# Two-part stores of the expert outputs, and weight conversion dealt out around each g in the FFN

## The chip, the cores and the metric

The kernel runs on 1 core of one Trainium2 chip. The metric is the device time of one execution in microseconds (us). The engines are named as in the profile: PE (TensorE matmul), PEld (TensorE weight load), DVE (VectorE), ACT (ScalarE), POOL (GpSimd), SP (SyncE, which only issues transfers here).

## The reference

Three layers follow each other on 2304 tokens of width 512.

```python
def phi(x):                                   # attention, 4 x 8 heads, 576 positions, head width 64
    proj = x @ w_phi                          # to 128 features
    proj = proj - max(abs(proj))
    return concat([exp(proj), exp(-proj)])
num = phi(q) @ (phi(k).T @ v); den = phi(q) @ sum(phi(k)) + 1e-6
x = num / den                                 # 2304 x 512

e_idx = argmax(x @ w_gate)                    # one of 8 experts for each token
for e in range(8):                            # expert stage, hidden width 1024
    h = maximum(x[mask] @ w1[e], 0)
    out[mask] = gate_w * sigmoid(x @ w_output_gate)[e] * (h @ w2[e])

h = x @ w_in                                  # FFN: 512 -> 2048 -> 512
out = (h * sigmoid(h)) @ w_out                # w_in and w_out come as float64
```

## The kernel before, in words

**Split operands.** Matrix products of the expert stage and the FFN are made from operands in two parts, a rounded high part (`h`) and a low part (`l`, the value minus its high part): high x high, high x low and low x high, three matmuls for one. The high part is an ACT copy into the rounded type (`F32R`), the low part a DVE subtraction.

**Expert stage** (class `Moe`). Tokens are sorted by expert into tiles of 256 slots, at most 16; a tile that is at most half full runs in a small form of 128. In this input 13 tiles run, numbers 0 to 12. For a tile t, `first` makes the hidden layer (96 matmuls, L754), `turn(t+1)` transposes the next tile's tokens, and `second` makes the output (96 matmuls, L781). `second_out` (small: the end of `second_small`) copies the result from PSUM into `y[t % 2]` by ACT, and `store` writes it by one DMA from SP's queue into the DRAM tensor `yT`, whose columns are tokens in expert order. Around that, `new_first` and `new_second` split the next expert's weights (ACT and DVE, L653 and L654), `scale` multiplies the gathered tokens (L683), `gather(t+2)` fetches tokens by an indirect DMA from POOL's queue (L670), and `side_work` converts one piece of the FFN's weights per tile. `after(t)` is called behind each tile: behind tile 8 (`SURE - 1`) it starts loading the first chunk of `yT`, behind tile 9 it splits that chunk and loads the next.

**FFN** (function `ffn`). `yT` is read in 6 chunks of 384 tokens, each twice, so there are 12 visits, v = 0 to 11. The hidden width of 2048 is cut into 4 quarters q. A step is a pair (v, q), 24 in all: steps 0 to 5 do quarter 0 for all chunks, steps 6 to 11 do quarters 1, 2 and 3 for visits 6 and 7 in turn, and then each of visits 8 to 11 does its three quarters. A step has 4 groups f, so there are 96 groups; they are called ups here, numbers 0 to 95. For each up, `up` runs 12 matmuls into a PSUM tile `fph` (L1000, two such tiles), ACT makes the sigmoid (L1002), DVE multiplies to g (L1003), ACT rounds g to `gh` (L1004), DVE makes `gl` (L1005). Behind each up, `down` runs the 9 matmuls (L1017) that belong to the up four places before. So PE alternates 12 and 9 matmuls.

The FFN's weights are float64 in DRAM, loaded as `raw` pieces of 128 x 512, and 24 pieces are converted inside the FFN: quarter 1 `i` (4 pieces), quarter 1 `o` (4), and so on to quarter 3, whose parts are written over the tiles of quarter 0 and bear their names, `i0` and `o0`. A piece takes an ACT magnitude (L888), five DVE instructions (`bits`, L894 to L898), a DVE addition (`add`, L903), an ACT copy (`high`, L906) and a DVE subtraction (`low`, L910). `fetch` issues the seven DVE instructions for one piece in one go, behind ups f = 0 and f = 2 of a step (in steps 7 to 10 behind f = 0, 2 and 3). Quarter q = 1 `i` is needed by up 24, `o` by the downs behind up 28, quarter 2 by ups 32 and 36, quarter 3 by ups 40 and 44. The program is in written order on each engine (`manual_schedule`), so an instruction that waits holds all that stands behind it on its engine. Visits are loaded into one staging tile `yst` by SP and split by `ready.next` (ACT L940, DVE L941, twice each per visit), behind f = 1 of the last step before a new visit.

Of the kernel before, what the change touches and what calls it, by code (L numbers as in the profile page):

```python
# [7 lines left out]
F32 = mybir.dt.float32  # L8
F32R = mybir.dt.float32r
# [5 lines left out]
ALU = mybir.AluOpType  # L15
# [586 lines left out]
class Moe:  # L602
# [14 lines left out]
    def open(self, c):  # L617
        tc = self.tc
        sp = c.enter_context(tc.tile_pool(name="m_s", bufs=1, reuse_waits="tile"))
        pt, ph, py = (c.enter_context(tc.tile_pool(name=n, bufs=1, space=PSUM, reuse_waits="tile")) for n in ("m_pt", "m_ph", "m_py"))  # L620
        self.hh, self.hl = (sp.tile([128, FC, TW], F32R, name=n) for n in ("hh", "hl"))
        self.y = self.ring(sp, "y", [128, KC, TW], 2)
# [107 lines left out]
    def second_small(self, t):  # L730
        nc, w, y = self.nc, self.w, self.y[t % 2]
# [10 lines left out]
        nc.scalar.copy(y[:, :, 0:128], q)  # L742
        self.store(t, 128)
# [24 lines left out]
    def store(self, t, n):  # L768
        co = self.nc.values_load(self.r["coff"][0:1, t:t + 1], engines=[ENG.SP], min_val=0, max_val=NTOK) if t else 0
        self.nc.sync.dma_start(out=self.yT[:, :, bass.ds(co, n)] if t else self.yT[:, :, 0:n], in_=self.y[t % 2][:, :, 0:n])  # L770

# [14 lines left out]
    def second_out(self, t):  # L786
        for g in range(2):
            self.nc.scalar.copy(self.y[t % 2][:, 2 * g:2 * g + 2], self.result[g])
        self.store(t, TW)

    def run(self, route, side_load, side_work, after):
        tc, nc = self.tc, self.nc
        side_load(0)
        side_load(1)
        self.first(0, self.y[1], (0,))
        route.slots(self.turned[0])
        self.first(0, self.y[1], (2, 4, 6))
        route.tokens(self.turned[1])
# [67 lines left out]
class Weights:  # L866
# [22 lines left out]

    def bits(self, pool, i, bufs):  # L890
        V, mag, (low, high) = self.nc.vector, self.mag[i], self.words(i)
        val = self.val[i] = pool.tile([128, 512], F32, name="val", bufs=bufs)
        bits = val.bitcast(I32)
        V.tensor_scalar(mag, mag, MAG_LO, MAG_HI, op0=ALU.max, op1=ALU.min)  # L894
        V.tensor_scalar(bits, mag.bitcast(I32), 3, 0x3FFFFFF8, op0=ALU.logical_shift_left, op1=ALU.bitwise_and)  # L895
        V.scalar_tensor_tensor(out=bits, in0=high, scalar=-0x40000000, in1=bits, op0=ALU.bitwise_and, op1=ALU.bitwise_or)  # L896
        V.tensor_scalar(mag.bitcast(I32), bits, -0x800000, None, op0=ALU.bitwise_and)  # L897
        V.scalar_tensor_tensor(out=mag, in0=low.bitcast(U32), scalar=2.0**-52, in1=mag, op0=ALU.mult, op1=ALU.mult)  # L898
        self.raw.pop(i)

    def add(self, i, eng):
# [11 lines left out]
class Ready:  # L913


    def __init__(self, nc, sp, yT):
        self.nc, self.sp, self.yT, self.parts = nc, sp, yT, {}
        self.pools = [sp, sp]
        self.st = sp.tile([128, KC, CN], F32, name="yst", bufs=1)

    def load(self, v):
        ch = v % NCH
        self.nc.sync.dma_start(out=self.st, in_=self.yT[:, :, ch * CN:(ch + 1) * CN])

    def room(self, v):
        self.parts[v] = [self.pools[v % 2].tile([128, KC, CN], F32R, name=n, bufs=1) for n in ("yh", "yl")]

    def next(self, v):

        self.room(v)  # L930
        self.split(v)
        if v + 1 < 2 * NCH:
            self.load(v + 1)

    def split(self, v):
        st = self.st
        yh, yl = self.parts[v]
        for kc in range(0, KC, 2):
            s = slice(kc, kc + 2)
            self.nc.scalar.copy(yh[:, s], st[:, s])  # L940
            self.nc.vector.tensor_sub(yl[:, s], st[:, s], yh[:, s].bitcast(F32))  # L941


def ffn(tc, r, weights, first_pool, fetch_pool, ready, out):

    nc = tc.nc
    V = nc.vector
    QC = GC // 4
    with ExitStack() as c, tc.manual_schedule():
        fp = c.enter_context(tc.tile_pool(name="f_f", bufs=1, reuse_waits="tile"))  # L950
# [6 lines left out]

        ready.pools[1] = sp
        rooms = [("i", 1, fp, "i1"), ("o", 1, wp, "o1"), ("i", 2, wp, "i2"), ("o", 2, wp, "o2")]
# [7 lines left out]
        todo = [(n, q, p) for q in range(1, 4) for n in "io" for p in range(KC)]  # L967
        at = [0]

        def load(n):  # L970
            weights.load(*((sp, todo[n], 1) if n % 3 == 2 else (fetch_pool, todo[n], 2)))

        def fetch():

            n = at[0]
            at[0] += 1
            if n + 1 < len(todo):
                weights.magnitude(sp, todo[n + 1], 3)
            if 2 <= n < len(todo) + 2:
                weights.high(todo[n - 2])  # L980
            if n < len(todo):
                weights.bits(sp, todo[n], 3)
                if n + 3 < len(todo):
                    load(n + 3)
            if 1 <= n < len(todo) + 1:
                weights.add(todo[n - 1], V)
            if 2 <= n < len(todo) + 2:
                weights.low(todo[n - 2], V)

        gts, accs = {}, {}  # L990

        def up(v, q, f):
# [10 lines left out]
            V.tensor_mul(g, p, g)  # L1003
            nc.scalar.copy(gh, g)  # L1004
            V.tensor_sub(gl, g, gh.bitcast(F32))  # L1005

        def down(v, q, f, i):
# [21 lines left out]
        steps += [(NCH + v, q) for v in range(2, NCH) for q in range(1, 4)]  # L1029
        first = {}  # L1030
        for n, (v, q) in enumerate(steps):
            first.setdefault(v, n)
        ready.next(1)
        load(2)
        for n, (v, q) in enumerate(steps):
            if n == NCH + 1:
                room("i", 3, first_pool, "i0")
                room("o", 3, first_pool, "o0")
            for f in range(QC):
                up(v, q, f)  # L1040
                if n == 0 and f == QC - 1:
                    weights.magnitude(sp, todo[0], 3)
                    fetch()
                if n and f in ((0, 2, 3) if NCH < n < NCH + 5 else (0, 2)):
                    fetch()
# [9 lines left out]
def build(tc, qT, kT, v, w_phi, w_gate, w_ogate, w1, w2, w_in, w_out, out, dbg=None):  # L1055
    nc = tc.nc
    with ExitStack() as c:
        cp = c.enter_context(tc.tile_pool(name="consts", bufs=1))
        dr = c.enter_context(tc.tile_pool(name="dram", bufs=1, space=bass.MemoryType.DRAM))
        xs = dr.tile([NTOK, XW], F32, name="xs")  # L1060
        yT = dr.tile([128, KC, NTOK + TW], F32, name="yT")
        k = make_consts(tc, cp)
# [8 lines left out]
        with ExitStack() as e:  # L1071
            with ExitStack() as m:
# [49 lines left out]
                def after(t):  # L1122
                    if t == SURE - 1:
                        cs.close()
                        yp = e.enter_context(tc.tile_pool(name="f_y", bufs=1, side="right", reuse_waits="tile"))
                        ready.append(Ready(nc, yp, yT))
                        ready[0].load(0)
                        ready[0].room(0)
                        ready.append(yp)
                        for p in range(2):  # L1130
                            weights.load(yp, ("i", 1, p), 2)
# [9 lines left out]
            with tc.using_default_side("left"):  # L1141
                ffn(tc, r, weights, ep, ready[1], ready[0], out)
        if dbg is not None:
            for n, a in dbg.items():
                nc.sync.dma_start(out=a, in_={**r, "xs": xs, "yT": yT}[n])

# [56 lines left out]
```

## Time and profile before

| what | value |
|---|---|
| median of 3 runs | 908.86 us (905.67 to 909.38) |
| the profiled execution, its own time | 907.69 us |
| its span, first to last instruction | 905.7 us |
| expert stage, from its first second-layer matmul to the last store's issue | about 200 to 477 us |
| FFN, first matmul to the end | 480.27 to 905.7 us |
| mean granted TensorE clock | 0.979 |

The time of an execution is longer than its span by what lies outside the first and the last instruction (2.0 us here). Times in the rows further down count from the start of the span.

### The profile page before, as it was taken

The numbers are of one execution on the slowest core, as the hardware profiler recorded it, in microseconds if no ns is written. First come the engines' busy times: TensorE is split into PE (matmuls) and PEld (weight loads), VectorE is DVE, ScalarE is ACT, GpSimd is POOL, SyncE is SP. The second block draws the span as 40 slices with busy tenths as digits, with TensorE's granted clock in tenths as the row PEclk, the third lists the DMA queues.
The fourth block names the chain that finished last, engine by engine and source line by source line (L and its number), as shares of the span: only waits on it lengthen the run. The fifth ranks groups of instructions, "written<-read, shape, count | busy, mean of one in ns | idle before, by whom it ended". The sixth has DMA issues, their size and how long they took to land. (4 is left out here: it accounts for less than half of the span.)

```text
span 905.7 us, 19488 instructions
## 1 busy us (share of the span) xinstructions
PE 851.0 (94%) x7908; PEld 764.8 (84%) x7908; DVE 525.7 (58%) x954; ACT 381.5 (42%) x715; POOL 76.1 (8%) x84
## 2 busy tenths in 40 slices
PE   7999989797999899999998999999799999999996
PEld 5888777687998889998987898888688989989895
DVE  5776677473379887437254777778864333333321
ACT  5556556531256666336254454453333232322220
POOL 0000024331000000011000000000001101010001
PEclk9999999998999999999998999999999999999999
DMA  4545255427247777427412333233201010100000
GB/s 143 154 120 146 77 179 166 113 51 279 71 143 265 252 249 254 147 59 245 142 41 83 119 105 116 82 105 92 71 1 70 35 36 35 35 24 12 12 24 35
DMA packets 47029, 99.40 MB, mean 110 GB/s; under 512 B 6592, under 2 KB 34880, under 8 KB 45120
## 3 DMA queue, kind: packets, MB, share of 16 engines
q1 hardware_dynamic: 43072, 85.16, 29.4%
q0 software_dynamic: 3840, 12.65, 4.6%
q8 instruction: 77, 1.26, 0.6%
q14 instruction: 40, 0.33, 0.1%
HBM read 82.55 MB, written 15.24 MB: 108 GB/s over the span
## 5 line engine op out<-in xcount | busy, mean ns | idle before, releaser
L1003 DVE TENSOR_TENSOR g<-fph,g 128x384 f32<-128x384 f32 x96 | 53.3, 555 | 123.8 <-ACT g L1002 123.8
L1002 ACT ACTIVATE g<-fph 128x384 f32<-128x384 f32 x96 | 47.1, 491 | 139.9 <-PE fph L1000 137.7
L1004 ACT CAST gh<-g 128x384 fp32r<-128x384 f32 x96 | 49.3, 513 | 125.3 <-DVE g L1003 125.3
L754 PE MATMUL ph<-xh,w1h 128*128 128x256 f32 x288 | 82.7, 287 | 6.7 <-PEq L813 6.0
L1005 DVE TENSOR_TENSOR gl<-g,gh 128x384 fp32r<-128x384 f32 x96 | 53.7, 560 | 55.7 <-ACT gh L1004 55.7
L754 PE MATMUL ph<-xl,w1h 128*128 128x256 f32 x288 | 82.1, 285 | 0.3 <-DVE xl L697 0.3
L754 PE MATMUL ph<-xh,w1l 128*128 128x256 f32 x288 | 81.9, 284 | 0.0
L781 PE MATMUL py<-hh,w2h 128*128 128x256 f32 x288 | 81.2, 282 | 0.0
L781 PE MATMUL py<-hl,w2h 128*128 128x256 f32 x288 | 80.4, 279 | 0.0
L781 PE MATMUL py<-hh,w2l 128*128 128x256 f32 x288 | 80.4, 279 | 0.0
L1000 PE MATMUL fph<-yh,i0h 128*128 128x384 f32 x192 | 66.6, 347 | 6.5 <-PEq L857 4.2
L1000 PE MATMUL fph<-yh,i0l 128*128 128x384 f32 x192 | 66.0, 344 | 3.2 <-DVE i0l L910 3.2
L1000 PE MATMUL fph<-yl,i0h 128*128 128x384 f32 x192 | 65.8, 343 | 0.0
L125 DVE TENSOR_REDUCE pmx<-pj 128x6 f32<-128x768 f32 x48 | 45.6, 950 | 32.9 <-PE pj L120 32.8
L754 PEld LDWEIGHTS ph<-xh,w1h 128*128 128x128 f32 x288 | 56.1, 195 | 7.7 <-issue 7.3
L146 PEld LDWEIGHTS pv<-v,E 128*64 128x64 f32 x1152 | 42.4, 139 | 17.5 <-issue 9.1
L1017 PE MATMUL fpo<-o0h,gl 128*128 128x512 f32 x144 | 57.1, 397 | 0.0
L1017 PE MATMUL fpo<-o0h,gh 128*128 128x512 f32 x144 | 57.0, 396 | 0.0
L146 PE MATMUL pv<-v,E 128*64 128x65 f32 (+1 forms) x1152 | 50.4, 234 | 6.8 <-ACT E L134 6.8
L1017 PE MATMUL fpo<-o0l,gh 128*128 128x512 f32 x144 | 56.8, 395 | 0.0
L754 PEld LDWEIGHTS ph<-xl,w1h 128*128 128x128 f32 x288 | 56.1, 195 | 0.5 <-DVE xl L697 0.5
L754 PEld LDWEIGHTS ph<-xh,w1l 128*128 128x128 f32 x288 | 56.1, 195 | 0.0
(256 smaller groups left out, 2076.0 us busy)
## 6 DMA issues: line engine op xcount, KB each, us to landing
w1s<-in_w SPq DMA_DIRECT2D x7, 2048.0 KB, 10.0
w2s<-in_w SPq DMA_DIRECT2D x7, 2048.0 KB, 8.1
yst<-yT SPq DMA_DIRECT2D x12, 768.0 KB, 5.1
raw<-in_w_in SPq DMA_DIRECT2D x16, 512.0 KB, 3.8
raw<-in_w_out SPq DMA_DIRECT2D x16, 512.0 KB, 3.6
v<-in_v SPq DMA_DIRECT2D x8, 650.0 KB, 3.9
raw<-in_k SPq DMA_DIRECT2D x24, 192.0 KB, 2.9
raw<-in_q SPq DMA_DIRECT2D x24, 192.0 KB, 4.1
```

The costliest lines, as they stand in the source:

```text
L125: V.tensor_reduce(mx, p, AX.X, ALU.max, apply_absolute_value=True)
L146: nc.tensor.matmul(pv[f:f + 64, s, o:o + n], E[:, i, j, s, f:f + 64], v1[:, c:c + n], start=i == 4 and s == 0, stop=i == 8 and s == 1,)
L754: nc.tensor.matmul(p[:, f, :], w[a][:, fs], b[:, kc, :], start=kc == 0 and n == 0, stop=kc == KC - 1 and n == 2)
L781: nc.tensor.matmul(self.result[d // 2][:, d % 2, :], w[a][:, fs], b[:, f, :], start=f == 0 and n == 0 and d % 2 == 0, stop=f == FC - 1 and ...
L1000: nc.tensor.matmul(p, a[:, kc, fs], b[:, kc, :], start=kc == 0 and n == 0, stop=kc == KC - 1 and n == 2)
L1002: nc.scalar.activation(g, p, AF.Sigmoid)
L1003: V.tensor_mul(g, p, g)
L1004: nc.scalar.copy(gh, g)
L1005: V.tensor_sub(gl, g, gh.bitcast(F32))
L1017: nc.tensor.matmul(p, a[:, s], b[:, f, :], start=q < 2 and f == 0 and n == 0, stop=done and n == 2)
```

## The change

The expert stage splits its result itself: `leave` writes the high part by an ACT copy and the low part by a DVE subtraction, both from PSUM, into a pair of tiles `yph` and `ypl` (one pair for all tiles, where there were two tiles `y`), and `store` writes them by two DMAs into two DRAM tensors. The FFN loads the two parts of a visit straight into `yh` and `yl` (two pairs), by two DMAs from POOL's queue, at the start of the step behind the last use of the visit before the previous; it splits nothing. The seven DVE instructions of a weight piece are counted as 11 units (1 for a `tensor_scalar`, 2 for the others), and each up from the fifth on issues 4 units between its g and its gl and 4 behind its gl.

```diff
 def second_out(self, t):
     for g in range(2):
-        self.nc.scalar.copy(self.y[t % 2][:, 2 * g:2 * g + 2], self.result[g])
+        self.leave(self.result[g], slice(2 * g, 2 * g + 2), TW)
     self.store(t, TW)
+def leave(self, p, s, n):
+    yh, yl = (y[:, s, 0:n] for y in self.y)
+    self.nc.scalar.copy(yh, p)
+    self.nc.vector.tensor_tensor(out=yl, in0=p, in1=yh.bitcast(F32), op=ALU.subtract)
 def store(self, t, n):
-    self.nc.sync.dma_start(out=self.yT[:, :, bass.ds(co, n)] if t else self.yT[:, :, 0:n], in_=self.y[t % 2][:, :, 0:n])
+    for y, yT in zip(self.y, self.yT):
+        self.nc.sync.dma_start(out=yT[:, :, bass.ds(co, n)] if t else yT[:, :, 0:n], in_=y[:, :, 0:n].bitcast(F32))
...
 # class Ready: next() and split() are gone
     def load(self, v):
-        self.nc.sync.dma_start(out=self.st, in_=self.yT[:, :, ch * CN:(ch + 1) * CN])
+        for y, yT in zip(self.parts[v], self.yT):
+            self.nc.gpsimd.dma_start(out=y, in_=yT[:, :, ch * CN:(ch + 1) * CN])
...
 # ffn
+    QUOTA = 4
+    def conversion():
+        for n in range(len(todo) + 2):
+            if n < len(todo):
+                weights.magnitude(sp, todo[n], 2)
+            if n >= 2:
+                weights.high(todo[n - 2])
+            if 1 <= n < len(todo) + 1:
+                weights.add(todo[n - 1], V)
+                yield 2
+            if n < len(todo):
+                yield from weights.bit_steps(sp, todo[n], 3)
+                load(n + 3)
+            if n >= 2:
+                weights.low(todo[n - 2], V)
+                yield 2
+    def fetch(until):
+        done[1] += until
+        while done[0] < done[1]:
+            done[0] += next(fetches, 1000)
     def up(v, q, f):
         nc.scalar.copy(gh, g)
+        if v or q:
+            fetch(QUOTA)
         V.tensor_sub(gl, g, gh.bitcast(F32))
+        if v or q:
+            fetch(QUOTA)
...
+    loads = {max(n for n, (a, _) in enumerate(steps) if a == v - 2) + 1: v for v in range(2, 2 * NCH)}
     for n, (v, q) in enumerate(steps):
+        if n in loads:
+            ready.room(loads[n])
+            ready.load(loads[n])
         for f in range(QC):
             up(v, q, f)
-            if n and f in ((0, 2, 3) if NCH < n < NCH + 5 else (0, 2)):
-                fetch()
-            if f == 1 and v > 0 and n == first.get(v + 1, 0) - 1:
-                ready.next(v + 1)
...
 # build, after(t)
     if t == SURE - 1:
+        for v in range(2):
+            ready[0].room(v)
         ready[0].load(0)
-        ready[0].room(0)
     if t == SURE:
-        ready[0].split(0)
         ready[0].load(1)
```

On DVE, in step 1 of the FFN, the order before is this (`g` and `gl` of an up, a whole piece, the next up's `g`; the last rows are a visit's split):

```order
L1005 TENSOR_TENSOR gl_10421<-g_10435,gh_10420 128x384
L894 TENSOR_SCALAR mag_10410<-mag_10410 128x512
L895 TENSOR_SCALAR val_10442<-mag_10410 128x512
L896 SCALAR_TENSOR_TENSOR val_10442<-raw_7335,val_10442 128x512
L897 TENSOR_SCALAR mag_10410<-val_10442 128x512
L898 SCALAR_TENSOR_TENSOR mag_10410<-raw_7335,mag_10410 128x512
L903 TENSOR_TENSOR val_10412<-mag_10408,val_10412 128x512
L1003 TENSOR_TENSOR g_10478<-fph_10465,g_10478 128x384
L1005 TENSOR_TENSOR gl_10464<-g_10478,gh_10463 128x384
L941 TENSOR_TENSOR yl_10484<-yst_7329,yh_10483 128x768 x2
```

With the change DVE has this in the same step (L1011 makes g, L1015 gl, L906 to L914 are `bits`, L920 `add`, L927 `low`):

```order
L1011 TENSOR_TENSOR g_10575<-fph_10562,g_10575 128x384
L920 TENSOR_TENSOR val_10544<-mag_10510,val_10544 128x512
L906 TENSOR_SCALAR mag_10581<-mag_10581 128x512
L908 TENSOR_SCALAR val_10585<-mag_10581 128x512
L1015 TENSOR_TENSOR gl_10561<-g_10575,gh_10560 128x384
L910 SCALAR_TENSOR_TENSOR val_10585<-raw_10394,val_10585 128x512
L912 TENSOR_SCALAR mag_10581<-val_10585 128x512
L914 SCALAR_TENSOR_TENSOR mag_10581<-raw_10394,mag_10581 128x512
L1011 TENSOR_TENSOR g_10616<-fph_10603,g_10616 128x384
```

Between one up's g and the next there were up to eight other instructions or a split; now there are seven at most, of which three stand ahead of `gl`.

On POOL, behind tile 8 of the expert stage, stands this before (the branch on whether tile 9 runs, and tile 9's gather for tile 11):

```order
L844 UNCONDITIONAL_BRANCH
L856 COMPARE_AND_BRANCH
L650 COMPARE_AND_BRANCH
L650 UNCONDITIONAL_BRANCH x2
L670 DMA xg_2846<-xs,tok 128x516 x2
```

And this with the change (`yTh` and `yTl` are the two DRAM tensors, L942 is `Ready.load`):

```order
L852 UNCONDITIONAL_BRANCH
L942 DMA yh<-yTh 128x4x384
L942 DMA yl<-yTl 128x4x384
L864 COMPARE_AND_BRANCH
L650 COMPARE_AND_BRANCH
L650 UNCONDITIONAL_BRANCH x2
L670 DMA xg_2847<-xs,tok 128x516 x2
```

The two loads of the first chunk have moved from SP's queue to POOL's, ahead of the gather for tile 11.

## Rows read from the trace of the kernel before

**Rows 1.** Page, part 1: busy us (share of the span) and instructions.

```profile
span 905.7 us, 19488 instructions
PE 851.0 (94%) x7908; PEld 764.8 (84%) x7908; DVE 525.7 (58%) x954; ACT 381.5 (42%) x715; POOL 76.1 (8%) x84
```

**Rows 2.** Timeline of PE: start, us, engine, line, operation [idle before <-releaser].

```profile
495.02 0.34 PE L1000 MATMUL fph<-yh,i0h 128*128 128x384 f32 x1
...
511.91 0.34 PE L1000 MATMUL fph<-yh,i0h 128*128 128x384 f32 x1
...
541.39 0.33 PE L1000 MATMUL fph<-yh,i0h 128*128 128x384 f32 x1
...
648.07 0.34 PE L1000 MATMUL fph<-yh,i0h 128*128 128x384 f32 x1
...
659.70 0.34 PE L1000 MATMUL fph<-yh,i0h 128*128 128x384 f32 x1
```

**Rows 3.** Chain that ended last: start, us, line, instructions.

```profile
661.97 2.09 PE fpo L1017 x9
...
664.06 2.11 PE fph L1000 x12
```

**Rows 4.** Waits of PE, 484 to 662 us: total, times, longest.

```profile
PE fph L1000 <- DVE g L1003: 3.8, 6, 1.1
PE fph L1000 <- DVE i0l L910: 3.2, 2, 2.4
PE fph L1000 <- ACT i0h L906: 1.6, 1, 1.6
```

**Rows 5.** Stretches: length, busy us of each engine, clock, DMA share, GB/s.

```profile
290.00:310.00 20.00, 18.32 (x173) 18.17 (x172) 19.27 (x36) 11.82 (x23) 1.89 (x2) 1.00 0.69 235
...
640.00:660.00 20.00, 14.09 (x57) 11.15 (x56) 15.88 (x31) 6.81 (x14) 0.00 (x0) 0.83 0.17 53
```

**Rows 6.** Timeline of DVE around one whole piece.

```profile
505.68 0.56 DVE L1005 TENSOR_TENSOR gl<-g,gh 128x384 fp32r<-128x384 f32 x1 [0.58 <-ACT gh L1004]
506.16 0.42 DVE L894 TENSOR_SCALAR mag<-mag 128x512 f32<-128x512 f32 x1
...
510.08 0.55 DVE L1003 TENSOR_TENSOR g<-fph,g 128x384 f32<-128x384 f32 x1
```

**Rows 7.** Groups by line: count, busy us, mean ns, idle before.

```profile
L941 DVE TENSOR_TENSOR yl<-yst,yh 128x768 fp32r<-128x768 f32 x24 | 21.9, 955 | 12.2 <-ACT yh L940 12.2
...
L697 DVE TENSOR_TENSOR xl<-pt,xh 128x512 fp32r<-128x512 f32 x24 | 15.3, 680 | 1.0 <-ACT xh L696 1.0
```

**Rows 8.** Page, part 6: transfers, KB each, median us to landing.

```profile
yst<-yT SPq DMA_DIRECT2D x12, 768.0 KB, 5.1
raw<-in_w_in SPq DMA_DIRECT2D x16, 512.0 KB, 3.8
...
yT<-y SPq DMA_DIRECT2D x9, 512.0 KB, 4.2
...
xg<-xs,tok POOLq DMA_INDIRECT x30, 3.8
```

**Rows 9.** POOL's gathers, and one beside DVE: line view, timelines.

```profile
L670 POOL DMA_INDIRECT xg<-xs,tok x30: 945/947/1122, 173.2 to 451.4; - x30
...
218.71 1.07 POOL L670 DMA_INDIRECT xg<-xs,tok  x1 [12.11 <-PEq L813]
...
218.48 0.88 DVE L683 TENSOR_SCALAR xg<-xg 128x512 f32<-128x512 f32 x2 [6.96 <-PEq L813]
```

**Rows 10.** Timelines of POOL, SP and DVE around tiles 8 to 11.

```profile
388.43 0.95 POOL L670 DMA_INDIRECT xg<-xs,tok  x1 [20.77 <-PE pt L694]
...
404.64 0.64 SPq L923 DMA_DIRECT2D yst<-yT  x1
...
419.81 0.87 DVE L683 TENSOR_SCALAR xg<-xg 128x512 f32<-128x512 f32 x2
...
427.72 1.28 DVE L697 TENSOR_TENSOR xl<-pt,xh 128x512 fp32r<-128x512 f32 x2
```

More of the change, by code (lines that the diff above doesn't have):

```diff
@@ L621, in open @@
         self.hh, self.hl = (sp.tile([128, FC, TW], F32R, name=n) for n in ("hh", "hl"))
-        self.y = self.ring(sp, "y", [128, KC, TW], 2)
+        self.y = [sp.tile([128, KC, TW], F32R, name=n) for n in ("yph", "ypl")]
         self.hs = sp.tile([128, FE], F32, name="hs")
@@ L730, in second_small @@
     def second_small(self, t):
-        nc, w, y = self.nc, self.w, self.y[t % 2]
+        nc, w = self.nc, self.w
         p = self.result[0].rearrange("p a n -> p (a n)")
@@ L741, in second_small @@
                 nc.tensor.transpose(q[:, d, :], self.hs[:, d * 128:(d + 1) * 128], self.k["ident"])
-        nc.scalar.copy(y[:, :, 0:128], q)
+        self.leave(q, slice(0, KC), 128)
         self.store(t, 128)
@@ L794, in run @@
         side_load(1)
-        self.first(0, self.y[1], (0,))
+        tmp = self.hs.rearrange("p (g n) -> p g n", n=TW)
+        self.first(0, tmp, (0,))
         route.slots(self.turned[0])
-        self.first(0, self.y[1], (2, 4, 6))
+        self.first(0, tmp, (2, 4, 6))
         route.tokens(self.turned[1])
@@ L890, in bits, with bit_steps @@
     def bits(self, pool, i, bufs):
+        for _ in self.bit_steps(pool, i, bufs):
+            pass
+    def bit_steps(self, pool, i, bufs):
         V, mag, (low, high) = self.nc.vector, self.mag[i], self.words(i)
@@ L894, in bits @@
         V.tensor_scalar(mag, mag, MAG_LO, MAG_HI, op0=ALU.max, op1=ALU.min)
+        yield 1
         V.tensor_scalar(bits, mag.bitcast(I32), 3, 0x3FFFFFF8, op0=ALU.logical_shift_left, op1=ALU.bitwise_and)
+        yield 1
         V.scalar_tensor_tensor(out=bits, in0=high, scalar=-0x40000000, in1=bits, op0=ALU.bitwise_and, op1=ALU.bitwise_or)
+        yield 2
         V.tensor_scalar(mag.bitcast(I32), bits, -0x800000, None, op0=ALU.bitwise_and)
+        yield 1
         V.scalar_tensor_tensor(out=mag, in0=low.bitcast(U32), scalar=2.0**-52, in1=mag, op0=ALU.mult, op1=ALU.mult)
         self.raw.pop(i)
+        yield 2
     def add(self, i, eng):
@@ L917, in __init__, with room, ffn @@
         self.nc, self.sp, self.yT, self.parts = nc, sp, yT, {}
-        self.pools = [sp, sp]
-        self.st = sp.tile([128, KC, CN], F32, name="yst", bufs=1)
+    def room(self, v):
+        self.parts[v] = [self.sp.tile([128, KC, CN], F32R, name=n, bufs=2) for n in ("yh", "yl")]
     def load(self, v):
         ch = v % NCH
-        self.nc.sync.dma_start(out=self.st, in_=self.yT[:, :, ch * CN:(ch + 1) * CN])
[L925 to L944, printed above, removed]
+        for y, yT in zip(self.parts[v], self.yT):
+            self.nc.gpsimd.dma_start(out=y, in_=yT[:, :, ch * CN:(ch + 1) * CN])
+def ffn(tc, r, weights, first_pool, ready, out):
     nc = tc.nc
@@ L956, in ffn @@
         )
-        ready.pools[1] = sp
         rooms = [("i", 1, fp, "i1"), ("o", 1, wp, "o1"), ("i", 2, wp, "i2"), ("o", 2, wp, "o2")]
@@ L967, in ffn @@
         todo = [(n, q, p) for q in range(1, 4) for n in "io" for p in range(KC)]
-        at = [0]
         def load(n):
[L971 to L980, printed above, removed]
-            if n < len(todo):
-                weights.bits(sp, todo[n], 3)
-                if n + 3 < len(todo):
-                    load(n + 3)
[L985 to L988, printed above, removed]
+            if n < len(todo):
+                weights.load(sp, todo[n], 3)
+        def conversion():
[6 more added lines that the diff above has]
+                    weights.add(todo[n - 1], V)
+                    yield 2
+                if n < len(todo):
+                    yield from weights.bit_steps(sp, todo[n], 3)
+                    load(n + 3)
+                if n >= 2:
+                    weights.low(todo[n - 2], V)
+                    yield 2
+        fetches = conversion()
+        done = [0, 0]
+        def fetch(until):
+            done[1] += until
+            while done[0] < done[1]:
+                done[0] += next(fetches, 1000)
         gts, accs = {}, {}
@@ L1029, in ffn @@
         steps += [(NCH + v, q) for v in range(2, NCH) for q in range(1, 4)]
[L1030 to L1034, printed above, removed]
+        loads = {max(n for n, (a, _) in enumerate(steps) if a == v - 2) + 1: v for v in range(2, 2 * NCH)}
+        for n in range(3):
+            load(n)
         for n, (v, q) in enumerate(steps):
@@ L1038, in ffn @@
                 room("o", 3, first_pool, "o0")
+            if n in loads:
+                ready.room(loads[n])
+                ready.load(loads[n])
             for f in range(QC):
                 up(v, q, f)
-                if n == 0 and f == QC - 1:
-                    weights.magnitude(sp, todo[0], 3)
-                    fetch()
-                if n and f in ((0, 2, 3) if NCH < n < NCH + 5 else (0, 2)):
-                    fetch()
-                if f == 1 and v > 0 and n == first.get(v + 1, 0) - 1:
-                    ready.next(v + 1)
                 for i in range(CH if n else 0):
@@ L1060, in build @@
         xs = dr.tile([NTOK, XW], F32, name="xs")
-        yT = dr.tile([128, KC, NTOK + TW], F32, name="yT")
+        yT = [dr.tile([128, KC, NTOK + TW], F32, name=n) for n in ("yTh", "yTl")]
         k = make_consts(tc, cp)
@@ L1126, in after @@
                         ready.append(Ready(nc, yp, yT))
+                        for v in range(2):
+                            ready[0].room(v)
                         ready[0].load(0)
-                        ready[0].room(0)
-                        ready.append(yp)
-                        for p in range(2):
-                            weights.load(yp, ("i", 1, p), 2)
                     if t == 4:
@@ L1141, in build @@
             with tc.using_default_side("left"):
-                ffn(tc, r, weights, ep, ready[1], ready[0], out)
+                ffn(tc, r, weights, ep, ready[0], out)
         if dbg is not None:
             for n, a in dbg.items():
-                nc.sync.dma_start(out=a, in_={**r, "xs": xs, "yT": yT}[n])
+                nc.sync.dma_start(out=a, in_={**r, "xs": xs}[n])
 def kernel(**inputs):
```

## The prediction

> **What bounds the kernel now.** I read the page's first part, the timeline of PE through the FFN, the waits of PE there, and then DVE's timeline at the places that those waits name. PE is busy for 94% of the span and DVE for 58% [rows 1], so only time in which PE stands still, or runs at a lower clock, can be won. The FFN is where that can be seen, since its pattern is regular: 12 matmuls of an up, 9 of its downs. In the second half of the FFN a pair takes 2.09 + 2.11 = 4.20 us with nothing between [rows 3].
>
> In the first half it takes longer. Up 5 starts at 495.02, up 41 at 659.70 [rows 2]: 164.68 us for 36 pairs, 4.57 each. Inside that stretch, up 9 (511.91) to up 16 (541.39) is clean: 29.48 / 7 = 4.21 us. So 36 clean pairs would take 151.6 us, and 164.7 - 151.6 = **13.1 us** are lost there. The longest loss is up 40: 648.07 to 659.70 is 11.6 us, 7.4 too many. The waits of PE say why [rows 4]: it waits for g on DVE (a PSUM tile `fph` comes free only when g is made), and for the parts of `i0`, the last quarter's weights, whose conversion ends while PE already needs them. The waits that PE's rows show sum to 8.6 us; the rest is in matmuls that start late without a named wait, and in the clock: from 640 to 660 the granted clock is 0.83 of 2.4 GHz on average, so part of the stretch ran at the level of 1.2 GHz after PE had idled [rows 5]. Subtracting start times takes in all of it, so I use 13.1 and not 8.6.
>
> Both waits have one source. From the start of `gl` at 505.68 to the next g at 510.08 DVE needs 4.40 us, of which 0.48 is `gl` and 3.92 the seven instructions of a weight piece [rows 6]. A g that is ready meanwhile stands behind them. Each visit's split adds two subtractions of 0.955 us [rows 7]. In steps 8 to 10, three pieces a step need 3 x 3.92 us and four ups 4 x (0.55 + 0.48 + 0.58 of waiting for `gh`): 18.2 us against 16.8 for PE.
>
> **The change part by part.** *Splits.* 24 subtractions of 0.955 us leave DVE, 22.9 us in all, and ACT's copies with them. In their place the expert stage makes 9 x 2 + 4 = 22 subtractions from PSUM of 128 x 512; the same form costs 0.68 us there now (`xl`) [rows 7], so 15 us of DVE. They start when PE has ended a tile's second layer; PE then runs the next tile's first layer, 96 matmuls with two thirds of an up's columns, some 11 us at 2.11 / 12 us for a whole one [rows 3], before it needs DVE's `hl`. I take 0 for the path. Bounds: 0, and 15 us if none were hidden. The stretch in which this cover is thinnest is 290 to 310, where DVE is busy for 19.27 of 20 us [rows 5]; a third of tiles lying like that would cost 3 to 5 us.
>
> *Conversion.* 24 pieces of 11 units are 264 units, 8 per up: 33 ups, numbers 4 to 36. Per up DVE then has g 0.55, `gl` 0.48 and 8/11 x 3.92 = 2.85, together **3.88 us against PE's 4.21**. At most three instructions, about 1.5 us, now stand between an up's g and its `gl`, and as much again ahead of the next g, so the wait for `gh` (0.58) is covered and no g stands behind a whole piece. From the order of the changed kernel, the last part of `i0` is made behind up 33 and needed by up 40; now it is made behind up 39. All other quarters end 7 to 13 ups ahead. Six times a piece's `add` and first step follow directly on g, and the first step can wait for ACT's magnitude; with twice the 0.58 each that is 7 us over 33 ups, 0.2 us per up, and 3.88 + 0.2 stays under 4.21. So PE's waits go: **-13.1 us**. Bounds: nothing gained if DVE became the bound (below), and not more than 13.1, as the rest of the FFN has no gap.
>
> *Loads of the parts.* A visit is now 2 x 768 KB by POOL's queue, where SP fetched 768 KB in 5.1 us [rows 8]. A load starts when PE has left the visit before the previous, and for seven visits (2 to 8) it must land within the next step, four pairs, 16.8 us, and the downs behind the last up, 2.1, where there are some (all but the first). No such load stands in the trace of before. From below: twice 5.1 us and one POOL issue of 0.95 us [rows 9], 11 us. From above: a gather moves 128 x 516 floats, 264 KB, in 3.8 us [rows 8]; at that rate 768 KB take 11 us, and two in a row 22. I take 11 to 14: same bytes, same layout as the SP load, on 16 engines that are free for two thirds of this time. That lies inside the window, so it costs nothing.
>
> *POOL's queue and the stores.* The first load has to wait for tile 8's stores. SP could issue it at 404.64; on POOL it stands ahead of the gather for tile 11, which went out at 388.43 [rows 10]. So that gather goes out 20 to 25 us later, about 410, landing at 414. It is used by `scale` at 419.81 and, behind it, by the turn near 427 [rows 10]; slack 6 us to the first, 13 to the second. The second store of a tile stands behind DVE's subtraction on SP's queue; nothing that SP issues next is due before the middle of the following tile. One pair of output tiles instead of two: a store lands in 4.2 us [rows 8], the next write is 15 us or more behind. All 0.
>
> *Start of the FFN.* Three raw pieces are now loaded at its start and not ahead of it: 3.8 us to land [rows 8], first used behind up 4, some 10 us on. 0.
>
> **Sum.** 907.7 (the profiled execution) - 13.1 = 894.6. The three runs' median, 908.9, lies 1.2 above that execution, so I forecast 908.9 - 13.1 = **895.8 us**.
>
> **The rivals.** (1) *The loads land late, and PE waits for `yh` at the start of seven steps.* With the upper bound of 22.1 us the first is 5.3 us late and six are 3.2 late: 24.5 us, 895.8 + 24.5 = 920. It decides from 18.3 us per load upwards (seven times over), eats the whole gain at about 20.5, and from 21 the kernel is slower by over 0.5%. For it: twice the bytes, POOL makes the transfers one after the other, and raw pieces share the engines. What DVE does beside POOL could add to it: the gather at 218.71 ran with two `tensor_scalar` from 218.48 beside it and took 1.07 us against 0.947 in the median [rows 9], so one such meeting cost 0.12. Against it: that price is small, and the SP load of half the bytes needs a third of the window. The Trainium skill ("SBUF — State Buffer", section Who interferes with whom) goes further: a DVE instruction in a two-port mode, such as a `tensor_scalar` from SBUF to SBUF, and GpSimd shut each other out for the whole instruction, the making of descriptors included. By that rule POOL would stand still through three of the seven DVE instructions of each piece and the loads would come later; the row agrees in direction, with 0.12 us. Chance 0.13, of which 0.06 slower.
>
> (2) *DVE becomes the bound.* If every up still lost the 0.58 us once, DVE would need 4.46 us per up, 0.25 more than PE, over 33 ups 8 us: 904. For it: 92% load in 33 ups in a row. Against it: the wait for `gh` is covered by 1.5 us of other work. With half of that, 900. Chance 0.12.
>
> (3) *The expert stage pays.* Late gathers or the 15 us of subtractions reach PE: 3 to 5 us likely if so, 899 to 901; all of it would be 911. Chance 0.07.
>
> (4) *The change does not do what it says*: the pieces are still late, because raw pieces or ACT hold them. Then PE waits at ups 24 to 40 as now: 905 to 909. The order speaks against it (7 ups of lead where there was one). Chance 0.03.
>
> **How the numbers follow.** The forecast, 892 to 898, has 0.65. The range of 0.8 reaches from 891.5, the forecast less the scatter of the runs shown (3.7 us from the fastest to the slowest), to 903.5, which takes in most of (2) and the likely part of (3). About 0.5%, 4.5 us, is what a measurement of this kernel can tell from no change. Faster by more than that: 0.65 + 0.10 of (2) + 0.05 of (1) + 0.04 of (3) = 0.84. Within: 0.02 + 0.02 + 0.02 + 0.03 = 0.09. Slower: 0.06 of (1) + 0.01 of (3) = 0.07.
>
> **What the profile of the changed kernel would show.** Up 5 to up 41 in about 152 us, no wait of PE for g or `i0`, and a clock of 1.00 throughout. DVE about 90% busy in steps 1 to 9 and g never more than 2 us behind its sigmoid. The two loads of a visit landing within 14 us. PE's tiles in the expert stage within 1 us of those before. I am wrong if PE waits for `yh` at the start of steps 2 to 7, if the pairs take more than 4.3 us with DVE busy throughout, or if PE stands at a turn near tile 10 or 11.

## The result, and the profile after

The changed kernel takes 894.5 us in the median of 4 runs (890.14 to 896.06), beside 907.33 us for the kernel before (4 runs). The ratio is 0.984, with a 95% interval from 0.981 to 0.987. The forecast of 895.8 us and its sign held. In a later set of 6 runs it was 894.69 us beside 911.1, ratio 0.983 (0.981 to 0.986).

The page's first part, to be held against [rows 1]: the span is 12.6 us shorter, and PE is busy for 4.2 us less, though it runs the same 7908 matmuls. POOL has 24 instructions more, the loads of the parts.

```profile
span 893.1 us, 19548 instructions
PE 846.8 (95%) x7908; PEld 765.2 (86%) x7908; DVE 514.2 (58%) x952; ACT 367.6 (41%) x691; POOL 95.8 (11%) x108
```

The timeline of PE at the first matmul of the FFN, at up 5 and at up 41, against [rows 2]:

```profile
482.88 0.66 PE L1008 MATMUL fph<-yh,i0h 128*128 128x384 f32 x1 [4.25 <-PEq L865]
...
498.04 0.34 PE L1008 MATMUL fph<-yh,i0h 128*128 128x384 f32 x1
...
648.70 0.34 PE L1008 MATMUL fph<-yh,i0h 128*128 128x384 f32 x1
```

Up 5 to up 41 (the column `difference` in the table further down) now takes 648.70 - 498.04 = 150.66 us against 164.68: **14.0 us** less, 4.185 per pair. From up 41 to the end of the span it is 893.1 - 648.70 = 244.4 against 905.7 - 659.70 = 246.0: **1.6 us** less. Most of that lies behind PE's last matmul:

```profile
898.52 0.40 PE L1017 MATMUL fpo<-o0l,gh 128*128 128x512 f32 x1
```

```profile
887.17 0.40 PE L1029 MATMUL fpo<-o0l,gh 128*128 128x512 f32 x1
```

From the end of this matmul to the end of the span it takes 905.7 - 898.92 = 6.8 us before and 893.1 - 887.57 = 5.6 now, so 1.2 of the 1.6 us are there, and only 0.4 in PE's pairs. Run e8 tells what the 1.2 us hang on.

The FFN begins 2.6 us later (482.88 against 480.27). Of that, 2.15 us are there already at the first hidden layer of the expert stage, ahead of all changed code (188.12 against 185.97), and in the repeated run that layer starts at 185.88 and the FFN at 480.51. So most of the shift lies ahead of the changed code, and it is gone in the repeated run. From its first matmul to up 5 the FFN takes 0.4 us more (15.16 against 14.75; 14.93 in the repeated run). Together: 14.0 + 1.6 - 2.6 - 0.4 = 12.6. In this stretch of the FFN the waits of PE from DVE and ACT [rows 4] are all gone; the view has no row.

DVE between two ups, against [rows 6]. No g waits for a piece, and `gl` follows without a wait for `gh`:

```profile
547.04 0.56 DVE L1011 TENSOR_TENSOR g<-fph,g 128x384 f32<-128x384 f32 x1 [0.56 <-ACT g L1010]
547.51 0.42 DVE L908 TENSOR_SCALAR val<-mag 128x512 int32<-128x512 int32 x1
547.97 0.69 DVE L910 SCALAR_TENSOR_TENSOR val<-raw,val 128x512 int32<-128x512 int32 x1
548.69 0.43 DVE L912 TENSOR_SCALAR mag<-val 128x512 int32<-128x512 int32 x1
549.04 0.55 DVE L1015 TENSOR_TENSOR gl<-g,gh 128x384 fp32r<-128x384 f32 x1
549.50 0.68 DVE L914 SCALAR_TENSOR_TENSOR mag<-raw,mag 128x512 f32<-128x512 uint32 x1
550.11 0.69 DVE L927 TENSOR_TENSOR o1l<-val,o1h 128x512 fp32r<-128x512 f32 x1
551.23 0.56 DVE L1011 TENSOR_TENSOR g<-fph,g 128x384 f32<-128x384 f32 x1 [0.44 <-ACT g L1010]
```

The groups of DVE by form, from 500 to 600 us (count, busy us, mean ns, idle before). First the kernel before: DVE stood idle for 13.3 us ahead of `gl` in 23 ups. Now it never does; ahead of g it stands idle for 6.8 us in 24 ups, because PE and the sigmoid are not ready:

```profile
L1005 DVE TENSOR_TENSOR gl<-g,gh 128x384 fp32r<-128x384 f32 x23 | 12.8, 559 | 13.3 <-ACT gh L1004 13.3
```

```profile
L1015 DVE TENSOR_TENSOR gl<-g,gh 128x384 fp32r<-128x384 f32 x25 | 13.8, 552 | 0.0
L1011 DVE TENSOR_TENSOR g<-fph,g 128x384 f32<-128x384 f32 x24 | 13.3, 556 | 6.8 <-ACT g L1010 6.7
```

Two stretches, with the columns of [rows 5]: the granted clock from 640 to 660 us is 1.00, where it was 0.83, and the stretch that the prediction called thin is full (DVE 19.91 of 20 us).

```profile
290.00:310.00 20.00, 20.00 (x171) 20.00 (x171) 19.91 (x35) 12.79 (x24) 1.89 (x2) 0.99 0.72 238
640.00:660.00 20.00, 20.00 (x103) 18.17 (x102) 5.02 (x10) 4.66 (x10) 0.32 (x1) 1.00 0.00 0
```

The transfers of the parts on the page (KB each, median us to landing), and POOL around the first pair and two later ones:

```profile
yh<-yTh POOLq DMA_DIRECT2D x12, 768.0 KB, 5.3
yl<-yTl POOLq DMA_DIRECT2D x12, 768.0 KB, 6.8
```

```profile
406.89 0.81 POOL L942 DMA_DIRECT2D yh<-yTh  x1 [36.46 <-DMA yTh<-yph]
408.76 0.77 POOL L942 DMA_DIRECT2D yl<-yTl  x1 [1.06 <-DMA yTl<-ypl]
410.04 1.03 POOL L670 DMA_INDIRECT xg<-xs,tok  x1 [0.51 <-PE ph L714]
...
525.75 0.74 POOL L942 DMA_DIRECT2D yh<-yTh  x1 [15.30 <-PE fph L1008]
...
659.68 0.74 POOL L942 DMA_DIRECT2D yh<-yTh  x1 [82.14 <-PE fph L1008]
```

By these medians a pair is there some 7.5 us behind its first issue (0.74 and 6.8); the seven pairs that a step waits for (visits 2 to 8) took 7.3 to 9.1 us. And the gather for tile 11 goes out at 410.04.

### The profile page after: what moved, and what is told of

Same layout as the page of the kernel before. It is cut to its first block, busy times and chain, and to the rows that moved or that the text cites. A ratio compares the mean times of both kernels' runs of the same rounds, so it can differ in the third digit from the quotient of the medians.

```text
span 893.1 us, 19548 instructions
## 1 busy us (share of the span) xinstructions
PE 846.8 (95%) x7908; PEld 765.2 (86%) x7908; DVE 514.2 (58%) x952; ACT 367.6 (41%) x691; POOL 95.8 (11%) x108
## 3 DMA queue, kind: packets, MB, share of 16 engines
q0 software_dynamic: 16512, 31.52, 12.8%
## 5 line engine op out<-in xcount | busy, mean ns | idle before, releaser
L1011 DVE TENSOR_TENSOR g<-fph,g 128x384 f32<-128x384 f32 x96 | 53.5, 557 | 155.0 <-ACT g L1010 154.6
L1015 DVE TENSOR_TENSOR gl<-g,gh 128x384 fp32r<-128x384 f32 x96 | 53.4, 556 | 36.5 <-ACT gh L1012 36.5
```

## The experiments

Two ways of reading the gain stood against each other: that the splits of the visits and whole pieces together made DVE too slow, and the change needs both its parts; or that only the conversion counts. A third question came out of the first runs: how far DVE may fall behind before PE pays. The table holds every run; the starts of up 5 and up 41 are rows of PE's timeline, the FFN is from its first matmul to the end of the span. Medians are of several chips, so the ratio to the kernel before on the same chip is what compares them.

| kernel | median us | ratio (95%) | up 5, up 41 | difference | FFN |
|---|---|---|---|---|---|
| before | 907.33 | 1 | 495.02, 659.70 | 164.68 | 425.4 |
| changed | 894.5 | 0.984 (0.981-0.987) | 498.04, 648.70 | 150.66 | 410.2 |
| changed, repeated | 894.69 | 0.983 (0.981-0.986) | 495.44, 646.11 | 150.67 | 410.0 |
| e1 deal only | 897.41 | 0.985 (0.983-0.987) | 496.08, 648.03 | 151.95 | 412.5 |
| e2 parts only | 902.59 | 0.992 (0.991-0.994) | 495.49, 655.01 | 159.52 | 419.2 |
| e3 all behind gl | 896.52 | 0.985 (0.984-0.987) | 495.06, 649.02 | 153.96 | 413.3 |
| e4 all ahead of gl | 895.54 | 0.983 (0.982-0.985) | 500.00, 650.67 | 150.67 | 409.9 |
| e5 gl three times | 916.44 | 1.007 (1.005-1.010) | 495.76, 669.66 | 173.90 | 433.4 |
| e6 whole pieces early | 902.72 | 0.991 (0.989-0.994) | 498.93, 658.46 | 159.53 | 418.6 |
| e7 loads twice | 897.16 | 0.986 (0.983-0.989) | 499.55, 650.22 | 150.67 | 409.6 |
| e8 loads by SP | 895.35 | 0.983 (0.981-0.985) | 498.76, 649.42 | 150.66 | 410.9 |
| e9 odd visits elsewhere | 894.9 | 0.983 (0.981-0.985) | 498.86, 649.43 | 150.57 | 409.0 |
| e10 = e3, one fph | 907.23 | 0.999 (0.997-1.001) | 502.49, 660.53 | 158.04 | 424.3 |
| e11 = changed, one fph | 899.63 | 0.991 (0.988-0.994) | 498.84, 650.41 | 151.57 | 416.5 |

**e1, the conversion alone.** The kernel before with the changed kernel's `bit_steps`, `conversion` and `fetch`, and its own stores, loads and splits.

```diff
             nc.scalar.copy(gh, g)
+            if v or q:
+                fetch(QUOTA)
             V.tensor_sub(gl, g, gh.bitcast(F32))
+            if v or q:
+                fetch(QUOTA)
...
-                if n and f in ((0, 2, 3) if NCH < n < NCH + 5 else (0, 2)):
-                    fetch()
```

> The kernel before, with the conversion alone dealt out in 4 units around each gl; one store for each tile, one load for each visit and the splits of the visits as before. Theory (each edit alone gives only a part of the gain, since DVE needs both to stay below PE): in steps 1 to 6 DVE needs 4 x 3.99 us for the ups plus two subtractions of 0.955 us and up to 1 us of waiting for ACT's copies, 17.9 to 18.8 us against 16.8 of PE; six such steps lose 6.6 to 12 us, so 901 to 906 us. No wait of PE for i0; waits for g, once or twice a step in steps 1 to 6. Rival (the dealing out is the whole gain): 894 to 897 us. Second rival (the expert stage of the change costs 2 us): below 894 us.

The theory missed: 897.4 us, 0.985. Up 5 to up 41 loses 1.3 us where 6.6 to 12 were expected, and PE waits for g once in all:

```profile
PE fph L1018 <- DVE g L1021: 0.5, 1, 0.5
```

So with the conversion dealt out, the splits cost almost nothing; that part of the change alone brings 12.7 of the 14.0 us in this stretch. By the ratios of the whole kernels (0.985 and 0.984) e1 and the changed kernel cannot be told apart; the stretch tells them apart. The sum behind the miss took every microsecond that DVE needs above PE's 16.8 per step as paid at once. DVE does fall behind: g starts 1.9 us behind the last matmul of up 5 and 6.2 behind that of up 22, yet PE pays 0.7 us (up 23).

**e2, the parts alone.** The changed kernel, with the pieces issued whole, where the kernel before issues them (its lines with `fetch()` come back, the dealing goes).

> The changed kernel, but the conversion issued in whole pieces at the same places as in the kernel before (behind f = 0 and 2, in steps 7 to 10 behind 0, 2 and 3); nothing is dealt out. Theory: the waits that came from the splits go (four pairs of 4.6 to 4.8 us, some 3 us in all), those from three pieces in a step stay: two pairs of 5.5 us and one of 10 to 12 us ahead of up 41, 8 to 10 us together; 902 to 905 us, PE waiting for i0. Rival (less work on DVE is the whole gain): 894 to 897 us and no wait for i0.

As expected, 902.6 us. The pairs of 4.6 to 4.8 us at ups 16, 20, 24 and 28 are gone (all of ups 5 to 37 take 4.16 to 4.24), and what is left is the end: pairs of 4.88, 12.23 and 4.71 us at ups 38, 40 and 41, PE waiting for the last quarter:

```profile
PE fph L1002 <- DVE i0l L927: 3.6, 2, 2.8
PE fph L1002 <- ACT i0h L923: 1.6, 1, 1.6
PE fph L1002 <- DVE g L1005: 0.6, 1, 0.6
```

A part of what is left is the clock: behind the wait of 2.8 us the granted clock is 0.50, the level of 1.2 GHz, for some 5 us (the columns are those of [rows 5]).

```profile
650.70:656.00 5.30, 5.30 (x14) 4.43 (x15) 3.29 (x7) 2.11 (x4) 0.00 (x0) 0.50 0.01 2
```

Alone, the parts bring 5.2 us of the 14.0. The two edits overlap: 12.7 + 5.2 is more than 14.0, since the splits cost much less where no whole pieces stand beside them (1.3 us in e1).

**e3 and e4, all units on one side of `gl`.**

```diff
 # e3
             nc.scalar.copy(gh, g)
-            if v or q:
-                fetch(QUOTA)
             V.tensor_sub(gl, g, gh.bitcast(F32))
             if v or q:
-                fetch(QUOTA)
+                fetch(2 * QUOTA)
```

> The changed kernel, with all 8 units of an up behind its gl, and none between g and gl. Theory: the wait of gl for gh, 0.58 us, is uncovered again in every up; g 0.55 + 0.58 + gl 0.48 + 2.85 + 0.1 = 4.56 us against 4.19 of PE, 0.37 x 33 = 12 us if nothing else gives; 902 to 907 us, with waits of PE for g in ups 6 to 37 and none for i0. Rival (equal shares are what counts, their place beside gl not): 893 to 896 us.

> The changed kernel, with all 8 units of an up between its g and its gl, and none behind gl. Theory: the wait for gh is covered all the same, gl comes some 1.4 us later than in the changed kernel, and the downs that read it are four ups off; 893 to 896 us, no wait of PE. Rival (a late gl holds PE, or the next g stands behind it): over 898 us.

e4 behaves like the changed kernel in every number, with `gl` 2.7 to 5.2 us behind g: the place of `gl` is free. In e3 the wait for `gh` is back in every up, as DVE's timeline shows:

```profile
601.52 0.56 DVE L1013 TENSOR_TENSOR gl<-g,gh 128x384 fp32r<-128x384 f32 x1 [0.58 <-ACT gh L1012]
602.00 0.68 DVE L920 TENSOR_TENSOR val<-mag,val 128x512 f32<-128x512 f32 x1
```

But it costs 3.3 us and not 12. The pairs stay at 4.19 to 4.20 up to up 21 and take 4.38 in the mean from up 23 (570.68) to up 38 (636.35). DVE falls behind from up 5 on, and for the first 17 ups nobody pays. The last matmul and the g of ups 5 and 21:

```profile
496.97 0.34 PE L1008 MATMUL fph<-yh,i0l 128*128 128x384 f32 x1
...
564.07 0.34 PE L1008 MATMUL fph<-yh,i0l 128*128 128x384 f32 x1
```

```profile
498.97 0.55 DVE L1011 TENSOR_TENSOR g<-fph,g 128x384 f32<-128x384 f32 x1
...
570.08 0.55 DVE L1011 TENSOR_TENSOR g<-fph,g 128x384 f32<-128x384 f32 x1
```

g starts 1.7 us behind the end of the matmul in up 5 and 5.7 in up 21, so DVE loses 0.25 us per up.

**e5, gl three times** (a loop of three around `V.tensor_sub(gl, ...)` in ups 4 to 36).

> The changed kernel, but DVE makes gl three times over in ups 4 to 36 (two more subtractions of 0.48 us an up, the same values). New theory (two PSUM tiles fph let DVE fall behind by some 5 us before PE waits: 6.3 us from the end of an up to the start of the second next, less 0.5 for the sigmoid and 0.55 for g; only what exceeds that is paid): DVE needs 3.88 + 0.96 = 4.84 us an up against 4.19; 0.65 x 33 = 21.5, less 5.2, so 16 us more than the changed kernel, 911 us; first wait of PE for g near up 12. First theory (each us of DVE above PE's pace is paid): 21 us more, 916 us, waits from the first ups on.

Measured 916.4 us, the number of the first theory, and by a sum that fits neither as written. A repeated subtraction costs 0.59 us and not 0.48, since 598.63 to 600.29 is 1.66 for three:

```profile
598.63 1.74 DVE L1017 TENSOR_TENSOR gl<-g,gh 128x384 fp32r<-128x384 f32 x3
600.29 0.42 DVE L912 TENSOR_SCALAR mag<-val 128x512 int32<-128x512 int32 x1
```

The pairs take 4.95 us in the mean (512.54 to 661.17 for ups 9 to 39), 0.77 more than 4.185; 33 of them are 25.4 us, and 23.2 were paid. So some 2 us of lag went unpaid, not 5, and the first slow pair is up 9. This run alone does not tell the two theories apart.

**e10 and e11, one PSUM tile `fph` in place of two**, made to settle that.

```diff
-            for n, b in (("f_pa", 2), ("f_ph", 2), ("f_pb", 4))
+            for n, b in (("f_pa", 2), ("f_ph", 1), ("f_pb", 4))
```

> The kernel with all 8 units behind gl, and with one PSUM tile fph in place of two. The first step's ups follow each other without downs and so lose about 1.2 us each at its start, some 4 to 5 us; what counts here is the stretch from up 5 to up 41, 153.9 us with two tiles and 150.7 in the changed kernel. Theory (the second tile is what lets DVE fall behind unpaid, 2 to 3 us in all; with one tile a g may lag by only 2.09 - 0.60 - 0.55 = 0.94 us behind its sigmoid): 0.19 us x 33 = 6.3, less 1 at most, so 155.5 to 157 us, PE waiting for g in nearly every up from up 6 on. Rival (the room comes from elsewhere, such as the downs being four ups behind): 154 us as with two tiles.

> The changed kernel with one PSUM tile fph in place of two. Start as in the other kernel with one tile, 4 to 5 us more up to up 5. From up 5 to up 41: theory: g lags by over 0.94 us behind its sigmoid in two ups only (1.40 and 1.32 us with two tiles), so 150.7 to 152 us and two or three short waits for g; 898 to 901 us in all. Rival (DVE at 90% needs the second tile all the way): over 153 us.

With all units behind `gl`, one tile costs 158.04 - 153.96 = 4.1 us more, about one pair: the pairs are slow from up 5 on, not from up 23. (The 157 at the top of the forecast was 1 us short.) The changed kernel with one tile loses 0.9 us in this stretch, nearly all of it at ups 5 and 6, where its g lags most. Ahead of up 5 the two lose 6.9 and 5.6 us, where ups follow each other without downs. So the second tile is the room that DVE has: at most one pair of lag, of which 2 to 5 us went unpaid in these runs. The changed kernel hardly uses it; e3 lives on it, and by its lag e1 does too, though e1 was not run with one tile.

**e6, whole pieces, but early** (e2 with `f in (0, 2, 3)` in all steps from 1 on, and with the room for quarter 3's `i` made one step earlier).

> The changed kernel, with the conversion in whole pieces again, but three to a step (behind f = 0, 2 and 3) from step 1 on, so that the last part of i0 is made behind up 31 (33 in the changed kernel, 39 before). Theory (equal shares with gh's wait covered matter besides the early end): DVE needs 3 x 3.92 + 4 x 1.61 = 18.2 us a step against 16.75; 1.45 x 8.7 steps = 12.6, less 5.2 of room, so 7 us more than the changed kernel, 902 us, waits of PE for g, none for i0. Rival (all that counts is that i0 is made early): 893 to 897 us.

902.7 us, as the theory had it. No wait for `i0`, whose last part is now made behind up 31, but for g:

```profile
PE fph L1002 <- DVE g L1005: 6.3, 6, 1.1
```

A step takes 18.12 us (605.45 to 623.57, ups 29 to 33), which is what DVE's instructions add up to. So finishing early does not do it. What this kernel lacks against the changed one is the cover of `gh`'s wait, 4 x 0.58 us a step, and small shares.

**e7 and e8, the loads** (each load issued twice; and the loads by `nc.sync` in place of `nc.gpsimd`).

> The changed kernel, but each visit's two parts are loaded twice over, in a row on POOL's queue. In the changed kernel a pair lands 7.5 us behind its first issue. Theory: the second pair lands 14 to 16 us behind the first issue, inside the window of 16.8, or PE waits for less than 1 us at a few steps; 893 to 900 us. First rival of the prediction (a pair lands only just in time): over 920 us, with waits of 7 us for yh at seven steps.

> The changed kernel, but the two loads of a visit go out from SP's queue instead of POOL's; the gather for tile 11 no longer stands behind the first of them. Theory (the loads are hidden and the gather has some 5 us to spare): 893 to 897 us, FFN 410 us, the expert stage from its first hidden layer to the first matmul of the FFN 294 to 295 us as in the changed kernel, the gather for tile 11 about 20 us earlier, and no wait gone from PE. Rival (POOL's queue costs something): 1 to 3 us less in the expert stage, below 893 us.

In e7 the second pair goes out as the first one lands, and PE never waits for `yh`: up 5 to up 41 stays at 150.67. For visits 2 to 8 the last of the four loads lands 14 to 16 us behind the first issue, so inside the window of 16.8 that the prediction named.

```profile
527.26 0.87 POOL L942 DMA_DIRECT2D yh<-yTh  x1 [6.56 <-PE fph L1008]
528.12 0.74 POOL L942 DMA_DIRECT2D yl<-yTl  x1
532.76 0.74 POOL L942 DMA_DIRECT2D yh<-yTh  x1 [3.90 <-DMA yh<-yTh]
536.14 0.74 POOL L942 DMA_DIRECT2D yl<-yTl  x1 [2.64 <-DMA yl<-yTl]
```

It does lose in the expert stage. The gather for tile 11 goes out at 417.35, and PE stands for 1.3 us in tile 10's second layer, since `scale` for tile 11 waits for it on DVE and `hl` stands behind:

```profile
432.23 0.39 PE L788 MATMUL py<-hl,w2h 128*128 128x256 f32 x1 [1.34 <-DVE hl L764]
```

```profile
427.99 0.49 DVE L683 TENSOR_SCALAR xg<-xg 128x512 f32<-128x512 f32 x1 [6.69 <-DMA xg<-xs,tok]
```

In e8 that gather goes out at 392.08 and nothing gets faster: in the changed kernel POOL's queue has room (how much is worked out in the next section). The expert stage takes 296.6 us up to the first matmul of the FFN, where 294 to 295 were expected; runs with the same code there took 293.9 to 297.7, so this says nothing of the queue.

What e8 does change is the end. The FFN takes 410.9 us, and the second half is back at 895.1 - 649.42 = 245.7:

```profile
887.89 0.40 PE L1029 MATMUL fpo<-o0l,gh 128*128 128x512 f32 x1
```

From the end of this last matmul to the end of the span it is 895.1 - 888.29 = 6.8 us, as before the change, and up to it the second half takes what it takes in the changed kernel (238.87 us). In e1, which also loads by SP, the end takes 6.8 too; in all runs that load by POOL it takes 5.5 to 5.6 (5.9 in e7). So the queue of the loads is worth 1.2 us at the end of the program. In all of them the chain that ended last closes on POOL (889.09 + 1.20 in e8), and what follows takes 4.8 us with loads by SP and 3.6 with loads by POOL. The reason was not tried.

**e9, the high part of the odd visits from 3 on in another pool.**

> The changed kernel, but the high part of the odd visits from 3 on lies in the pool f_s, where both parts of the odd visits lay before, and not beside those of the even ones. Question: why the second half of the FFN (up 41 to the end) takes 244.4 us in the changed kernel and 246.0 before, with no wait in either. If it is the place of the odd visits' tiles in memory, their pairs are slower by 0.01 to 0.03 us and the second half takes 245 to 246 us, the FFN 411 us; if it is the splits or SP's loads beside PE, it stays at 244.4 us and 410 us.

The second half stays at 893.8 - 649.43 = 244.4 us, and up to PE's last matmul it takes 238.84 us (238.87 in the changed kernel, 239.22 before). That is the second answer of the forecast: the place of these tiles is not where the second half gained: 1.2 us come with POOL's loads, by e8. What the run showed instead is told last. No kernel of these beats the changed one: e4, e8 and e9 lie inside its interval.

## Why the prediction was right, step by step

The forecast of 13.1 us came from the stretch between up 5 and up 41, and there the mechanism held. That the medians differ by as much, 12.8 us, is partly luck: 2.5 us that were not forecast (0.9 and 1.6, below) are offset in this profile by a start of the FFN and first ups that are 3.0 us later, and the kernel before was at its lowest in this set (907.33 us, against 909.09 to 911.1 in the later ones). The repeated run gained 16.4 us. The lower end of the prediction's range is given as the forecast less 3.7, which would be 892.1 and not 891.5.

- **What bounds the kernel.** 13.1 us lost between up 5 and up 41, by comparison with clean pairs of 4.21. Measured gain there: 14.0. The step held; the 0.9 is the pace of the pairs (4.185), which was slower before even where nothing waited.
- **Splits removed.** Worth 1.3 us in this stretch when the conversion is dealt out (e1), 5.2 when it is not (e2). The prediction credited them and the pieces jointly and did not say which; e1 says it is mostly the pieces.
- **Conversion dealt out.** 3.88 us of DVE against 4.21 of PE: PE never waits, and g starts 1.4 us behind the end of its sigmoid at most, inside the 2 us that were named. DVE was busy for 84% to 93% of stretches of a step's length between 496 and 630 us. The early end alone would not have done it (e6); the cover of `gh`'s wait was worth 3.3 us (e3).
- **Subtractions in the expert stage.** Taken as 0, and 0 is what is seen: from the first hidden layer to the FFN's first matmul it takes 294.76 us (294.63 in the repeat) against 294.30. Runs with the same code in this stage took 293.9 to 297.7 us, though (e7, with other loads, apart), so a cost below some 3 us would not be seen. The thin stretch did fill up (DVE 19.91 of 20), and PE waits 1.0 us for `scale` at 276.89; 0.3 to 0.5 us are left of that at the stage's end.
- **Loads of the parts.** Mis-sized: 11 to 14 us a pair were taken, 7.3 to 9.1 were measured, since the second load runs beside the first instead of behind it. The first rival named 18.3 us as the point from which it decides; by its own windows (16.8 and 18.9 us) only the first of the seven steps would wait there, for 1.5 us, and all seven only above 18.9. e7, with twice the loads in 14 to 16 us, still showed no wait, but it did not reach that point either. The price from the gather's rate (22 us) was never near.
- **DVE beside POOL.** An issue on POOL takes 0.74 us at 525.75, with a `tensor_scalar` on DVE from 525.67 to 526.10, and 0.74 us at 659.68, with DVE idle at first. The longest of the 24 took 0.82. The exclusive lock that the Trainium skill describes ("SBUF — State Buffer", section Who interferes with whom) would, by an estimate from these times, have put 0.35 us on top of the first (525.75 to 526.10). No load's issue here shows that, and the measurement decides. An indirect transfer does lose beside DVE: in the kernel before, the scatter at 714.17 took 1.36 us with `gl` on DVE from 714.12 to 714.68, and the one at 710.68 took 0.97 with DVE idle.
- **POOL's queue.** The gather was forecast for about 410 and went out at 410.04. It was to land at 414, but it took 6.2 us and landed at 416.3; `scale` came to it at 420.76, so 4.5 of the 6 us of slack were there. e7 sent it out 9.3 us later than the repeated run of the changed kernel (417.35 against 408.03), 6.8 of them relative to the start of tile 10 (418.10 against 415.60), and there it took 10.6 us to land in place of 6.4. So it landed 11.0 us later against tile 10, `scale` started 6.8 later, and tile 10 took 25.3 us in place of 23.5. PE paid 1.8 us for 11.0: some 9 us were free on its path, of which `scale` used up the first 4.
- **The second rival** (DVE as the bound) was priced as 0.25 us per up over 33 ups, 8 us. Its condition, an uncovered 0.58 us, was made true by e3 and cost 3.3: DVE lost 0.25 us per up at first and 0.19 from up 23 on, 6 to 8 us in 33 ups, and 3 to 5 of that were absorbed by the second `fph` tile. That sum of the prediction was wrong, on the safe side.
- **The rest of the FFN** was taken as 0 and gained 1.6 us without a wait on either side. 1.2 us of it lie behind PE's last matmul and come with the loads on POOL's queue (e8); the prediction had no term for the end of the program. The other 0.4 us are pace of PE's pairs. They do not come from the queue of the loads, since e8 has them too; e1, with the old splits and places of tiles, lacks them.

## What to carry to other kernels

Where an engine feeds PE at a load close to PE's own pace, look at what stands between two of its urgent instructions before removing work: dealing out the same 264 units evenly brought 12.7 us, removing 23 us of other work brought 5.2. Put the filler where the engine would wait anyway (here between g and `gl`). A buffer more is a fixed credit of lag, not a rate: in e3 it hid a shortfall of some 0.2 us a round for some 17 rounds, and from then on PE went at DVE's pace.

## What was not expected of the hardware

PE's pace depends by about 1% on where the operands lie, with nothing waiting. In e9, whose only edit is the pool of the odd visits' `yh` (tiles behind it in that pool move too), the 12 matmuls of an up on visit 3 take 2.11 to 2.12 us and the 9 matmuls of the downs in step 7 take 2.05 us, where the repeated run of the changed kernel has 2.10 and 2.08. First e9, then the repeat, from the chain that ended last (start, us, line, count):

```profile
528.38 2.11 PE fph L1010 x12
...
532.59 2.12 PE fph L1010 x12
...
597.72 2.05 PE fpo L1031 x9
```

```profile
529.15 2.10 PE fph L1008 x12
...
598.32 2.08 PE fpo L1029 x9
```

In the kernel before, pairs of odd visits take 4.22 to 4.23 us and those of even ones 4.19 to 4.21 in steps 1 to 3, where none waits. In the changed kernel both take 4.19, and in e9, with the odd high parts back in their old pool, the pairs of step 3 take 4.21 to 4.22 again. So the place explains a part of the 0.9 us of pace in the first half. Whether it also explains the 0.4 us of the second is not shown: e9 moved only the high parts, and gained as much in some steps there as it lost in others. The reason for the dependence was not tried.
